# Start-up, v loads and low parts moved in a one-core attention and MLP kernel

## The chip, the cores and the metric

The kernel runs on one core of one Trainium2 chip. The metric is the device time of one execution in microseconds (us): the median over several runs. The engines of the core run side by side, each through its own queue in order: TensorE (PE, with its weight loads as PEld), VectorE (DVE), ScalarE (ACT), GpSimd (POOL) and SyncE (SP, which here only issues transfers, DMAs). They wait for one another by semaphores.

## What is computed

64 heads (8 batches of 8) of causal attention with a decay, of 576 positions and 64 dimensions each, then an MLP with a squared ReLU over the 4608 rows that result.

```python
scores = scale * np.matmul(q, k.transpose(0, 1, 3, 2))
log_f = np.log(np.clip(f, 0.0001, 1.0))
cum = np.cumsum(log_f, axis=-1)
decay = cum[:, :, :, None] - cum[:, :, None, :]
scores = np.where(causal, -1000000000.0, scores + decay)
scores = scores - np.max(scores, axis=-1, keepdims=True)
attn = np.exp(scores)
attn = attn / (np.sum(attn, axis=-1, keepdims=True) + 1e-09)
attn_out = np.matmul(attn, v)
x = attn_out.transpose(0, 2, 1, 3).reshape(B * S, H * D)
h = np.maximum(x @ w_in, 0.0)
out = h * h @ w_out                    # w_in 512 x 2048, w_out 2048 x 512
```

All of it is wanted in float32. The query's own sum `cum[q]` cancels in the softmax, so only the key's sum is carried, as extra rows of the operand k.

## The kernel before

**Heads and slots.** Each head is cut in six units (`UNITS`), a block of up to 128 keys by a stretch of queries. A slot is one unit of one head, and the main loop (`for n in range(-2 * NU, last_slot + 1)`) writes a slot at a time: the unit's scores, the product with v of the unit two slots back (`av_part`), then what the tables `events` and `fins` hold for this slot and its two halves, and between them a share of the MLP (`fill`) and of the weights' conversion (`cv`). `in_order` then binds PE, ACT, DVE and POOL to the order in which the instructions were written; SP's transfers after the start-up follow it too, each behind those before it.

**Row maxima.** Softmax needs each query's maximum before its scores are raised. Six maximum units per head (`max_units`) run one head ahead of the scores: a matmul over q and k rounded to float32r (`r2`, `kl0`, 66 rows: 64 dimensions and the high and low half of the sums), then a reduction on DVE out of the same PSUM bank (L384). `MAXIMA` gives their slots. For heads 0 to 9 (`NWHOLE`) the maxima are turned by TensorE and copied as a row of the whole float32 operand `whole` (tile `rl`) by ACT (`turn_maxima`, L411); the scores of these heads are plain float32 matmuls (L423). From head 10 on the scores are two float32r matmuls (L425, L428) of a rounded part (tile `rk`) and a low part (tile `rl`), made by `prep` in four parts. In heads 10 to 19 DVE subtracts the low parts (L329 for k, L333 for q), from head 20 on POOL does.

**The banks.** Maximum units and scores share PSUM banks. While the MLP's first chunks run, the maxima have no banks of their own and take turns with the scores, for a time on two banks; a second maximum unit then cannot start before DVE has read the first.

**Sums.** `decay` clips f, takes Ln on ACT, sums along each of 64 rows by one DVE scan (L167), rounds the sums to `ch` (L170) and subtracts for `cl` (L171). Head 0's two rows go from there into its two operands by transfers (L284); all 64 heads' rows go to DRAM (`cum_dr`, L176), and every later head loads its two rows from there (L286).

**Start-up.** PE runs 36 matmuls on a constant (`spin`, L768) until there is work; their result is not used. SP loads f, head 0's q and k (`rl`), a first weight tile. POOL's queue loads q and k of heads 0 and 1 a second time as float32r (`rk`, L292, which rounds them), and fills constant rows.

**Loads.** v of head h is loaded one head ahead (slot 2 of head h-1) into one of three buffers, and is first used in slot 2 of head h (L487). Weights come in 32 tiles of 512 KB, DEPTH 4 ahead of their conversion, which ACT and DVE share (L206, L211 on ACT; L230, L235, L238, L242, L217 on DVE). `RATES` says how many conversion steps a slot gets: 0.67 in the first slots before head 0, none in the last six of them, 0.93 and then 1.8 once heads run.

Of the kernel before, what the change touches and what calls it, by code (L numbers as in the profile page):

```python
# [9 lines left out]
F32 = mybir.dt.float32  # L10
# [4 lines left out]
ALU = mybir.AluOpType  # L15
# [19 lines left out]
def decay_attention_relu2_kernel(  # L35
# [77 lines left out]
    nc.vector.memset(turn[:, P:P + 2 * CW].bitcast(F32), 0.0)  # L113
    nc.vector.tensor_copy(out=eye_r, in_=eye)

# [37 lines left out]
    cum, cums = [], []  # L153

    def load_f():
        nc.sync.dma_start(out=fr[:NH, 0, :], in_=f)

    def decay():
        ft, zt, ct = (fr[:NH, i, :] for i in range(3))
        nc.vector.memset(zt, 0.0)  # L160
        constant_rows(nc.vector, rounded[0])
        nc.vector.tensor_scalar(ft, ft, 1e-4, 1.0, ALU.max, ALU.min)
        nc.scalar.activation(out=ft, in_=ft, func=AF.Ln)
        warm_exp = wk.tile([P, 8], F32, name="tcol")
        nc.vector.memset(warm_exp[:, :1], 0.0)
        nc.scalar.activation(out=warm_exp[:, :1], in_=warm_exp[:, :1], func=AF.Exp)
        nc.vector.tensor_tensor_scan(ct, zt, ft, 0.0, ALU.add, ALU.add)  # L167
        chl = wk.tile([P, 2, S], F32R, name="qkraw", bufs=1)
        ch, cl = chl[:, 0, :], chl[:, 1, :]
        nc.vector.tensor_copy(out=ch[:NH], in_=ct)  # L170
        nc.vector.tensor_tensor(out=cl[:NH], in0=ct, in1=ch[:NH].bitcast(F32), op=ALU.subtract)  # L171
        cum.extend(x.bitcast(F32) for x in (ch, cl))
        cums.append(chl[:NH].bitcast(F32))
# [105 lines left out]

    def load_cum(h, k, r=D):  # L280

        if h == 0:
            for i, c in enumerate(cum):
                nc.sync.dma_start(out=f32(k[r + i:r + i + 1, :S]), in_=c[h:h + 1])  # L284
        else:
            nc.sync.dma_start(out=f32(k[r:r + 2, :S]), in_=cum_dr[h])  # L286

# [7 lines left out]

    def load_whole(h):

        x = state[h]["whole"] = whole[h % 2]
        nc.sync.dma_start(out=x.raw[:D], in_=qk[h])
        if cum:  # L300
            load_cum(h, x.k, D + 1)
# [368 lines left out]

    RATES = (0.67, 0, 0.93, 1.8)
    LAG = 2
# [72 lines left out]
    for h in range(NH):  # L745
        split = h >= NWHOLE
        if split:
            at((h - 2) * NU + LOAD, 0, load, h)
            for part in range(4):
                at((h - 1) * NU + SPLIT[part], 1, prep, h, part)  # L750
        else:
            if h > 1:
                at((h - 3) * NU + 3, 0, load_rounded, h)
                at((h - 2) * NU + 5, 1, load_whole, h)
        at((h - 1) * NU + VLOAD, 1, load_v, h)
        at((h - 1) * NU + VSPLIT, 1, split_v, h)
        for i, x in enumerate(MAXIMA[split]):
            at((h - 1) * NU + int(x), int(2 * x) % 2, max_unit, h, i)
        if not split:
            at((h - 1) * NU + (4 if h else 3), 0, turn_maxima, h)  # L760
# [9 lines left out]
    for i in range(12):  # L770
        at(i // 2 - NU, i % 2, spin, 1)
    spin(36)
    load_f()
    load_rounded(0)
    load_whole(0)
    constants()
    convert(1)
    decay()
    load_cum(0, rounded[0].k)
    load_cum(0, whole[0].k, D + 1)  # L780
    store_cum()
    convert(1)
    load_rounded(1, False)
    load_whole(1)
    load_cum(1, rounded[1].k)
    start = {i.name for i in tc.nc.cur_bb.bb.instructions}
    for n in range(-2 * NU, last_slot + 1):
# [15 lines left out]
        for do in events.get((n, 0), ()):  # L803
            do()
        wr = RATES[0] * (n < -NU) if n < -NU // 2 else RATES[1 if n < 0 else 2 if n < ready[0] else 3]
        cv(wr / 2)
# [50 lines left out]
```

## Time and profile before

| what | us |
|---|---|
| runs of the kernel | 1206.62, 1206.76, 1213.95 |
| median | 1206.76 |
| the profiled execution's own time | 1208.21 |
| its span, first to last instruction | 1206.5 |

The profile's page gives the busy time of each engine and its share of the span. The view of the waits has one row per pair of a waiting line and the one that released it: us in total, times, longest. The timeline has a row per instruction or run of like instructions: start, duration, engine, line, operation, out<-in, count, and in brackets the idle time before it with what ended it. A view of windows gives, for each stretch of the span, its length, each engine's busy time and count, then PEclk (the granted TensorE clock as a share of full speed), the busy share of the transfer engines, and GB/s. "L376" is a line of the kernel before; a step whose line moves keeps its name in words.

### The profile page before, as it was taken

Reading aid. Unit: us, or ns where it says so; the run is one execution under the profiler, and the core shown is the slowest. Engines: PE = TensorE matmul, PEld = TensorE weight load, DVE = VectorE, ACT = ScalarE, POOL = GpSimd, SP = SyncE. Lnnn points to the kernel's source line nnn. Section 1 sums busy time; section 2 is a strip of 40 time slices with the busy share of each in tenths; the row PEclk is TensorE's granted clock in tenths of the full one; section 3 lists DMA queues with packets and bytes.
Section 4 is the critical chain, followed back from the end, with each engine's and each line's share of the span. In section 5 each row is a group of like instructions: output and inputs, shape, how many; then the busy total and the mean of one; then the engine's idle time right before and its main releaser. Section 6 shows DMA issues by size and latency. Waiting matters only on the chain. (4 is left out here: it accounts for less than half of the span.)

```text
span 1206.5 us, 23195 instructions
## 1 busy us (share of the span) xinstructions
PE 1178.1 (98%) x7786; PEld 1040.9 (86%) x7786; DVE 784.9 (65%) x2096; ACT 684.6 (57%) x1716; POOL 316.9 (26%) x511
## 2 busy tenths in 40 slices
PE   8999999999999999999999999999999999999998
PEld 4667877789998989899999899988999899999997
DVE  5889987766766676666656667666666766543332
ACT  3765555546666566656565566666566666533232
POOL 2110000213434343422222343334333434200000
PEclk9999999999999999999999999999999999999999
DMA  7785722221212121111110212112121112000000
GB/s 204 194 209 165 196 54 46 74 67 35 51 42 60 42 55 43 50 42 35 36 50 17 59 38 54 38 43 59 42 54 36 47 42 59 12 28 18 1 19 18
DMA packets 109798, 73.33 MB, mean 61 GB/s; under 512 B 90720, under 2 KB 90720, under 8 KB 109680
## 3 DMA queue, kind: packets, MB, share of 16 engines
q1 hardware_dynamic: 108880, 68.90, 22.4%
q0 software_dynamic: 800, 2.95, 1.1%
q8 instruction: 62, 1.02, 0.4%
q14 instruction: 56, 0.46, 0.1%
HBM read 58.71 MB, written 9.87 MB: 57 GB/s over the span
## 5 line engine op out<-in xcount | busy, mean ns | idle before, releaser
L621 PE MATMUL bank<-w,gh 128*128 128x512 f32 x1152 | 413.5, 399 | 0.0
L591 PE MATMUL bank<-xh,w 128*128 128x256 f32 x2304 | 331.6, 286 | 5.3 <-ACT r L606 5.1
L591 PEld LDWEIGHTS bank<-xh,w 128*128 128x128 f32 x2304 | 300.1, 189 | 16.8 <-ACT r L606 9.3
L456 DVE TENSOR_TENSOR pl<-p,ph 128x320 fp32r<-128x320 f32 (+4 forms) x288 | 175.4, 610 | 200.6 <-ACT ph L455 195.1
L621 PEld LDWEIGHTS bank<-w,gh 128*128 128x128 f32 x1152 | 217.5, 189 | 37.9
L621 PE MATMUL bank<-w,gl 128*128 128x512 f32 x576 | 227.1, 394 | 0.2 <-DVE gl L609 0.2
L455 ACT CAST ph<-p 128x320 fp32r<-128x320 f32 (+4 forms) x288 | 119.4, 415 | 162.0 <-POOL p L442 119.2
L607 DVE TENSOR_TENSOR g<-r 128x256 f32<-128x256 f32 x288 | 124.3, 432 | 102.0 <-ACT r L606 101.7
L442 POOL TENSOR_SCALAR_AFFINE_SELECT p<-p 128x128 f32<-128x128 f32 (+1 forms) x240 | 85.9, 358 | 396.1 <-ACT p L440 328.2
L606 ACT ACTIVATE r<-bank 128x256 f32<-128x256 f32 x288 | 109.7, 381 | 137.1 <-PE bank L591 124.5
L591 PE MATMUL bank<-xl,w 128*128 128x256 f32 x1152 | 184.8, 283 | 0.0
L440 ACT ACTIVATE p<-bank 128x320 f32<-128x320 f32 (+4 forms) x288 | 111.2, 386 | 117.9 <-PE bank L428 105.9
L384 DVE CUSTOM_DVE_ANT_0 bank<-bank,mz 128x256 f32<-128x256 f32 (+4 forms) x320 | 133.6, 431 | 50.6 <-PE bank L376 50.2
L609 DVE TENSOR_TENSOR gl<-g,gh 128x256 fp32r<-128x256 f32 x288 | 139.1, 483 | 34.4 <-PE bank L621 1.0
L591 PEld LDWEIGHTS bank<-xl,w 128*128 128x128 f32 x1152 | 158.5, 191 | 0.2 <-DVE xl L577 0.2
L608 ACT ACTIVATE gh<-r 128x256 fp32r<-128x256 f32 x288 | 120.4, 418 | 9.2
L376 PE MATMUL bank<-rk 66*128 66x320 f32 (+4 forms) x384 | 109.1, 314 | 13.4 <-DVE tcol L384 8.4
L621 PEld LDWEIGHTS bank<-w,gl 128*128 128x128 f32 x576 | 109.2, 190 | 15.0 <-DVE gl L609 1.7
L428 PE MATMUL bank<-rl 128*128 128x320 f32 x324 | 95.1, 294 | 0.0
L425 PE MATMUL bank<-rk 67*128 67x320 f32 x324 | 93.4, 288 | 0.0
L376 PEld LDWEIGHTS bank<-rk 66*128 66x128 f32 (+1 forms) x384 | 67.1, 181 | 30.4 <-DVE tcol L384 12.8
L466 PE MATMUL bank<-pl,vh 128*65 128x320 f32 (+4 forms) x336 | 91.3, 272 | 0.0
(97 smaller groups left out, 1478.8 us busy)
## 6 DMA issues: line engine op xcount, KB each, us to landing
qkraw<-in_qk SPq DMA_DIRECT2D x54, 288.0 KB
v<-in_v SPq DMA_DIRECT2D x64, 160.0 KB
out<-osb SPq DMA_DIRECT2D x36, 256.0 KB
den<-rdr SPq DMA_DIRECT2D x62, 144.0 KB
w<-in_w_in SPq DMA_DIRECT2D x16, 512.0 KB
w<-in_w_out SPq DMA_DIRECT2D x16, 512.0 KB
rk<-tcol SPq DMA_DIRECT2D x216, 0.5 KB
rl<-in_qk SPq DMA_DIRECT2D x10, 288.0 KB
```

Of the source, the lines that this page charges most:

```text
L376: nc.tensor.matmul(ps[:m, :n], st["r2"][:D + 2, q0:q0 + m], st["kl0"][:D + 2, k0:k0 + n], start=True, stop=True,)
L384: nc.vector.tensor_tensor_reduce(out=ps[:m, :n], in0=ps[:m, :n], in1=mz[:m, mo:mo + n], op0=ALU.add, op1=ALU.min, scale=-1.0, scalar=init, ...
L428: nc.tensor.matmul(ps[:kn, :n], st["l2"][:, k0:k0 + kn], st["r1"][:, q0:q1], start=False, stop=not added,)
L440: nc.scalar.activation(out=p[:kn, :n], in_=ps[:kn, :n], func=AF.Exp, scale=SCALE)
L455: nc.scalar.copy(out=ph[:kn, :n], in_=p[:kn, :n])
L456: nc.vector.tensor_tensor(out=pl[:kn, :n], in0=p[:kn, :n], in1=ph[:kn, :n].bitcast(F32), op=ALU.subtract,)
L591: nc.tensor.matmul(ph[:, :T], w[:, s, cc], x[:, cc, :], start=(cc == 0 and k == 0), stop=(cc == NCC - 1 and k == 2),)
L606: nc.scalar.activation(out=r, in_=ph[:, :T], func=AF.Relu)
L607: nc.vector.tensor_tensor(out=g, in0=r, in1=r, op=ALU.mult)
L608: nc.scalar.activation(out=gh, in_=r, func=AF.Square)
L609: nc.vector.tensor_tensor(out=gl, in0=g, in1=gh.bitcast(F32), op=ALU.subtract)
L621: nc.tensor.matmul(po, g[:, ts], w[:, s], start=(fc == 0 and k == 0), stop=(fc == NF - 1 and k == 2),)
```

## The change

Five things are changed.

1. *Head 0's start.* q and k of head 0 are no longer loaded twice; ACT rounds them out of the float32 tile (two copies of 64 rows). f is loaded on 66 partitions: ACT's queue brings head 0's row twice more, onto partitions 64 and 65. The clip, Ln, scan and rounding run on 66 partitions, and one DVE operation on the last two writes head 0's two sum rows in place: `ch * sign + sum`, with sign 0 on partition 64 (the sum, rounded on writing) and -1 on 65 (its low half).
2. *Head 1's sums* and head 0's float32 rows come from chip by transfers, not through DRAM.
3. *Fewer spins*: 20 for 36. The rounding of the unit matrix `eye_r` stands behind the clip. Conversion steps that stood before head 0's maxima stand behind them (RATES 0 until three slots before head 0, then 1.0).
4. *v sooner*: heads 2 to 9 load v two heads ahead in place of one.
5. *Maxima ahead of low parts*: for heads from 10 on, where a maximum unit and a part of `prep` fall in the same half slot, the maximum unit is now written first.

```diff
-    nc.vector.tensor_copy(out=eye_r, in_=eye)
...
+    NR = NH + 2
+    signs = wk.tile([P, 8], F32, name="tcol")[:, :1]
...
         nc.sync.dma_start(out=fr[:NH, 0, :], in_=f)
+        nc.scalar.dma_start(out=fr[NH:NR, 0, :], in_=f[0:1].broadcast_to([2, S]))
 
     def decay():
-        ft, zt, ct = (fr[:NH, i, :] for i in range(3))
+        ft, zt, ct = (fr[:NR, i, :] for i in range(3))
+        x = rounded[0]
...
+        nc.vector.memset(signs[NH:NR], -1.0)
+        nc.vector.memset(signs[NH:NH + 1], 0.0)
         nc.vector.tensor_scalar(ft, ft, 1e-4, 1.0, ALU.max, ALU.min)
         nc.scalar.activation(out=ft, in_=ft, func=AF.Ln)
+        nc.vector.tensor_copy(out=eye_r, in_=eye)
+        nc.scalar.copy(out=x.k[:D, :S], in_=whole[0].k[:D, :S])
+        nc.scalar.copy(out=x.q[:D], in_=whole[0].q[:D])
...
-        nc.vector.tensor_copy(out=ch[:NH], in_=ct)
-        nc.vector.tensor_tensor(out=cl[:NH], in0=ct, in1=ch[:NH].bitcast(F32), op=ALU.subtract)
+        nc.vector.tensor_copy(out=ch[:NR], in_=ct)
+        nc.vector.scalar_tensor_tensor(
+            x.k[NH:NR, :S], ch[NH:NR].bitcast(F32), signs[NH:NR], ct[NH:NR], ALU.mult, ALU.add,
+        )
+        nc.vector.tensor_tensor(
+            out=cl[:NH], in0=ct[:NH], in1=ch[:NH].bitcast(F32), op=ALU.subtract,
+        )
...
-    RATES = (0.67, 0, 0.93, 1.8)
+    RATES = (1.0, 0.93, 1.8)
...
-            for part in range(4):
-                at((h - 1) * NU + SPLIT[part], 1, prep, h, part)
...
-        at((h - 1) * NU + VLOAD, 1, load_v, h)
+        if h:
+            at((h - (2 if 1 < h < NWHOLE else 1)) * NU + VLOAD, 1, load_v, h)
         at((h - 1) * NU + VSPLIT, 1, split_v, h)
         for i, x in enumerate(MAXIMA[split]):
             at((h - 1) * NU + int(x), int(2 * x) % 2, max_unit, h, i)
+        if split:
+            for part in range(4):
+                at((h - 1) * NU + SPLIT[part], 1, prep, h, part)
...
-    spin(36)
+    spin(20)
     load_f()
-    load_rounded(0)
-    load_whole(0)
+    state[0] = dict(r2=rounded[0].q, kl0=rounded[0].k, p={})
+    load_rounded(1, False)
+    load_whole(0, False)
+    convert(1)
     constants()
+    decay()
+    for i, c in enumerate(cum):
+        for x, r in (whole[0], D + 1), (rounded[1], D):
+            h = 0 if x is whole[0] else 1
+            nc.sync.dma_start(out=f32(x.k[r + i:r + i + 1, :S]), in_=c[h:h + 1])
     convert(1)
-    decay()
-    load_cum(0, rounded[0].k)
-    load_cum(0, whole[0].k, D + 1)
+    load_v(0)
+    load_whole(1, False)
+    load_cum(1, whole[1].k, D + 1, False)
     store_cum()
     convert(1)
-    load_rounded(1, False)
-    load_whole(1)
-    load_cum(1, rounded[1].k)
...
-        wr = RATES[0] * (n < -NU) if n < -NU // 2 else RATES[1 if n < 0 else 2 if n < ready[0] else 3]
+        wr = 0 if n < -NU // 2 else RATES[0 if n < 0 else 1 if n < ready[0] else 2]
```

PE's own order is the same in both kernels but for the 16 spins. On the others it moves. DVE at the start, before (`p` is the tile of the unit matrix, `xt` holds f and its sums, `rk` the rounded operand, `qkraw` the two halves of the sums):

```order
L114 CAST p<-p 128x128
L160 MEMSET xt_86 64x576
L141 MEMSET rk_79 32x576
L142 MEMSET rk_79 32x578
L143 MEMSET rk_79 64x2
L148 MEMSET rk_79 2x2
L162 TENSOR_SCALAR xt_86<-xt_86 64x576
L165 MEMSET tcol 128x1
L167 SCALAR_TENSOR_TENSOR xt_86<-xt_86 64x576
L170 CAST qkraw<-xt_86 64x576
L171 TENSOR_TENSOR qkraw<-xt_86,qkraw 64x576
L230 TENSOR_SCALAR wmag<-wmag 128x512
```

and DVE at the start now:

```order
L142 MEMSET rk_78 64x2
L147 MEMSET rk_78 2x2
L166 MEMSET tcol 2x1
L167 MEMSET tcol 1x1
L168 TENSOR_SCALAR xt_85<-xt_85 66x576
L170 CAST p<-p 128x128
L174 MEMSET tcol 128x1
L176 SCALAR_TENSOR_TENSOR xt_85<-xt_85 66x576
L179 CAST qkraw<-xt_85 66x576
L180 SCALAR_TENSOR_TENSOR rk_78<-qkraw,tcol,xt_85 2x576
L183 TENSOR_TENSOR qkraw<-xt_85,qkraw 64x576
L398 ISA bank_166,tcol<-bank_166,mz 128x256
```

The unit matrix went from the head of the queue to behind the clip, the two-row operation (L180) is new, and the weight's steps (L230 before) left the place between the sums and the first maximum (L398 is the reduction, L384 before). SP's queue at the start, before:

```order
L284 DMA rk_79<-qkraw 1x16x36 x2
L284 DMA rl<-qkraw 1x16x36 x2
L176 DMA cum_dr<-qkraw 64x1152
L195 DMA w_164<-in_w_out 128x1024
L299 DMA rl<-in_qk 64x1152
L286 DMA rl<-cum_dr 2x576
L286 DMA rk_80<-cum_dr 2x576
L306 DMA v<-in_v 128x5x64
L286 DMA rk_79<-cum_dr 2x576
```

and SP's queue at the start now:

```order
L799 DMA rl<-qkraw 1x16x36
L799 DMA rk_79<-qkraw 1x16x36
L799 DMA rl<-qkraw 1x16x36
L799 DMA rk_79<-qkraw 1x16x36
L209 DMA w_154<-in_w_out 128x1024
L320 DMA v<-in_v 128x5x64
L313 DMA rl<-in_qk 64x1152
L300 DMA rl<-qkraw 1x16x36 x2
L190 DMA cum_dr<-qkraw 64x1152
L209 DMA w_233<-in_w_in 128x1024
L209 DMA w_235<-in_w_out 128x1024
L297 DMA rk_78<-cum_dr 2x576
```

Head 1's rounded operand (`rk`) now gets its sums in the first four transfers rather than from DRAM behind a weight tile and q and k; the store to DRAM has gone back behind v, and the first load from it (L297) is head 2's. DVE in one of the heads 10 to 19, before:

```order
L607 TENSOR_TENSOR g<-r 128x256
L609 TENSOR_TENSOR gl<-g,gh 128x256
L329 TENSOR_TENSOR rl<-qkraw,rk_80 64x576
L384 ISA bank_2776,tcol<-bank_2776,mz 128x256
L384 ISA tcol 128x1
L384 ISA bank_2789,tcol<-bank_2789,mz,tcol 128x320
```

and the same place now:

```order
L621 TENSOR_TENSOR g<-r 128x256
L623 TENSOR_TENSOR gl<-g,gh 128x256
L398 ISA bank_2764,tcol<-bank_2764,mz 128x256
L398 ISA tcol 128x1
L343 TENSOR_TENSOR rl<-qkraw,rk_79 64x576
L398 ISA bank_2779,tcol<-bank_2779,mz,tcol 128x320
```

The low part of k (L329, now L343) stands between the first and the second maximum unit, where it stood ahead of both.

More of the change, by code (lines that the diff above doesn't have):

```diff
@@ L153, in decay_attention_relu2_kernel @@
     cum, cums = [], []
+    NR = NH + 2
+    signs = wk.tile([P, 8], F32, name="tcol")[:, :1]
     def load_f():
         nc.sync.dma_start(out=fr[:NH, 0, :], in_=f)
+        nc.scalar.dma_start(out=fr[NH:NR, 0, :], in_=f[0:1].broadcast_to([2, S]))
     def decay():
-        ft, zt, ct = (fr[:NH, i, :] for i in range(3))
+        ft, zt, ct = (fr[:NR, i, :] for i in range(3))
+        x = rounded[0]
         nc.vector.memset(zt, 0.0)
-        constant_rows(nc.vector, rounded[0])
+        constant_rows(nc.vector, x)
+        nc.vector.memset(signs[NH:NR], -1.0)
+        nc.vector.memset(signs[NH:NH + 1], 0.0)
         nc.vector.tensor_scalar(ft, ft, 1e-4, 1.0, ALU.max, ALU.min)
         nc.scalar.activation(out=ft, in_=ft, func=AF.Ln)
+        nc.vector.tensor_copy(out=eye_r, in_=eye)
+        nc.scalar.copy(out=x.k[:D, :S], in_=whole[0].k[:D, :S])
+        nc.scalar.copy(out=x.q[:D], in_=whole[0].q[:D])
         warm_exp = wk.tile([P, 8], F32, name="tcol")
@@ L278, in load, with load_cum @@
         raws[h] = raw
-    def load_cum(h, k, r=D):
-        if h == 0:
+    def load_cum(h, k, r=D, stored=True):
+        if stored:
+            nc.sync.dma_start(out=f32(k[r:r + 2, :S]), in_=cum_dr[h])
+        else:
             for i, c in enumerate(cum):
                 nc.sync.dma_start(out=f32(k[r + i:r + i + 1, :S]), in_=c[h:h + 1])
-        else:
-            nc.sync.dma_start(out=f32(k[r:r + 2, :S]), in_=cum_dr[h])
     def load_rounded(h, rows=True):
@@ L294, in load_rounded, with load_whole @@
             load_cum(h, x.k)
-    def load_whole(h):
+    def load_whole(h, rows=True):
         x = state[h]["whole"] = whole[h % 2]
         nc.sync.dma_start(out=x.raw[:D], in_=qk[h])
-        if cum:
+        if cum and rows:
             load_cum(h, x.k, D + 1)
```

## The prediction

> **What bounds the kernel now.** I read the page first, then the waits of TensorE, the windows by stage, the timeline of the start, and last the timeline around each wait.
>
> ```profile
> span 1206.5 us, 23195 instructions
> PE 1178.1 (98%) x7786; PEld 1040.9 (86%) x7786; DVE 784.9 (65%) x2096; ACT 684.6 (57%) x1716; POOL 316.9 (26%) x511
> PE bank L376 <- DVE tcol L384: 8.4, 8, 1.7
> PE bank L591 <- ACT r L606: 5.1, 8, 0.8
> PE bank L376 <- DMA rk<-cum_dr: 2.6, 1, 2.6
> PE bank L487 <- DMA v<-in_v: 2.0, 1, 2.0
> PE bank L487 <- ACT w L211: 1.2, 1, 1.2
> 27.00:77.00 50.00, 45.91 (x266) 31.22 (x265) 39.84 (x123) 39.15 (x95) 6.58 (x14) 1.00 0.79 191
> 97.00:262.00 165.00, 154.77 (x974) 129.71 (x973) 135.25 (x344) 90.44 (x219) 14.92 (x33) 0.99 0.38 103
> 262.00:1035.00 773.00, 767.53 (x5241) 701.22 (x5240) 519.32 (x1408) 475.12 (x1210) 280.55 (x423) 1.00 0.19 45
> ```
>
> TensorE is busy 1178.1 of 1206.5 us; its order stays as it is but for 16 spins, so the change can win only its idle 28.4 us, clock, and the time before its first useful matmul. From 262 us on it idles 5.5 us in 773, and nothing there is touched on its path. What can move lies in three places: the start, the early heads (4.1 us idle in 27 to 77), and heads 10 to 19 (10.2 us idle in 97 to 262, 8.4 of them maxima waiting for DVE).
>
> **The start.**
>
> ```profile
> 0.81 1.28 ACT L163 ACT_TABLE_LOAD   x1 [0.81 <-PEq L847]
> 1.70 9.89 PE L768 MATMUL bank<-mz 128*128 128x448 bf16 x36 [1.70 <-POOL mz L95]
> 2.47 0.54 DVE L160 MEMSET xt<- 64x576 f32 x1
> 4.58 0.63 DVE L162 TENSOR_SCALAR xt<-xt 64x576 f32<-64x576 f32 x1
> 5.24 0.68 ACT L163 ACTIVATE xt<-xt 64x576 f32<-64x576 f32 x1 [3.15 <-DVE tcol L165]
> 5.96 1.35 DVE L167 TENSOR_TENSOR_SCAN xt<-xt 64x576 f32<-64x576 f32 x1 [0.74 <-ACT xt L163]
> 7.34 0.47 DVE L170 CAST qkraw<-xt 64x576 fp32r<-64x576 f32 x1
> 7.62 3.52 PEld L768 LDWEIGHTS <-mz 128*128 128x128 bf16 x19 [0.22 <-issue]
> 7.84 1.31 SPq L284 DMA_DIRECT2D rk<-qkraw  x2
> 7.84 0.75 DVE L171 TENSOR_TENSOR qkraw<-xt,qkraw 64x576 fp32r<-64x576 f32 x1
> 8.04 0.68 ACT L206 ACTIVATE wmag<-w 128x512 f32<-128x512 f32 x1 [0.60 <-DMA w<-in_w_in]
> 11.74 0.35 PE L376 MATMUL bank<-rk 66*128 66x256 f32 x1 [0.15 <-DMA rk<-qkraw]
> 14.57 0.23 SPq L286 DMA_DIRECT2D rk<-cum_dr  x1
> 16.44 0.70 PE L423 MATMUL bank<-rl 67*128 67x320 f32 x2
> 19.73 0.50 PE L376 MATMUL bank<-rk 66*128 66x256 f32 x2 [2.59 <-DMA rk<-cum_dr]
> 27.73 0.67 PE L376 MATMUL bank<-rk 66*128 66x256 f32 x2
> 34.85 0.67 PE L376 MATMUL bank<-rk 66*128 66x256 f32 x2
> 2.00:3.00 1.00, 1.00 (x4) 0.46 (x3) 0.75 (x2) 0.09 (x1) 0.95 (x3) 1.00 0.91 198
> 7.00:8.00 1.00, 1.00 (x5) 0.39 (x4) 0.93 (x3) 0.43 (x2) 0.78 (x7) 1.00 0.12 14
> ```
>
> The first maximum starts at 11.74, when head 0's sum rows land, 3.1 us after the second of two transfers was issued (its half of 1.31 us begins when L171 ends, 8.59). Now DVE writes these rows. When, is a chain. VectorE no longer waits for the unit matrix first, so its four fills, begun at 2.47 before, begin at about 1.1; from there to the clip it took 4.58 - 2.47 = 2.1, and two tiny fills more make it free at about 3.5. f must have landed: its 147 KB lead the queue, at 198 GB/s from 2.0 they are through by 2.75, and w's transfer, whose bytes end by about 7.1 (the share falls to 0.12), lands at 8.04, 0.9 later. So f lands at about 3.65, and before 4.58 in any case. The extra row pair on ScalarE's queue is tiny and lands with it. A wait is added here: ScalarE now waits for f ahead of Ln's table load, which ran at 0.81 for nothing before. So 3.65, table 1.28, Ln 0.68, scan 1.35, rounding 0.47, the two-row operation, with gaps of 0.03: 7.54 before that operation. No row shows it; by length it lies between L170 (0.47) and L171 (0.75), both 576 long; I take 0.75 as it has two tensor operands like L171: 8.3. Two rows for 64 save nothing, since I take time by length. With f at 4.55 it is 9.2.
>
> ScalarE's two roundings of q and k have Ln's form, 0.68 each: from 5.65 to 7.0, if head 0's float32 q and k are in. They stand behind f in the queue (442 KB, 5 us); shared evenly with w they land with it, 8.0, and the roundings end at 9.4. Exp's table and the weight's first step follow on ScalarE, which is next needed 3.8 us after the first maximum.
>
> The spins: 19 weight loads in 3.52 is 0.19 each, so 16 fewer end 3.0 earlier, at 8.6. That is later than 8.3, so the first maximum starts at 8.6 to 8.75 and gains **3.0**; bounds 2.3 (9.4) and 3.1. The unit matrix (DVE's wait for Ln covers it) and the three conversion steps behind head 0's maxima (they run while TensorE turns the maxima and scores, 16.44 to 19.73 before) cost nothing; without that cover they would delay head 1's first reduction by up to 1.5. One reload of 295 KB on POOL's queue is gone.
>
> Then 4.7 us of maxima, as 11.74 to 16.44: first score at 13.45. Its float32 rows and head 1's come by four transfers issued from 7.5 to 10.7; at 3.1 each the last lands by 13.1. Head 1's maxima, which waited 2.59 for a row from DRAM, follow the score at 14.1 without a wait: **2.6**; bounds 1.5 and 2.6.
>
> SP has the store and the read from DRAM further back, so head 2 pays instead: its row is issued once w, v, q and k, two sums and the store are through, about 17.7 by the issue times and some 250 GB/s. A row like it took 5.1 (issued 14.57, used 19.73): 21 to 22.8, when head 2's maxima want it at 14.1 + 7.1 = 21.2 (a head takes 34.85 - 27.73 = 7.1). I charge **0.7**; bounds 0 and 1.6. Head 1's v, three weight tiles behind, lands just about when wanted, and is in this charge.
>
> **The clock.**
>
> ```profile
> 21.50:24.50 3.00, 3.00 (x12) 2.00 (x11) 2.89 (x12) 1.41 (x4) 0.91 (x2) 0.50 0.62 204
> 243.50:246.50 3.00, 3.00 (x14) 2.76 (x13) 1.08 (x6) 0.80 (x2) 0.00 (x0) 0.50 0.03 0
> ```
>
> For some 3.4 us each TensorE has half its clock, the only two such stretches. Each follows a wait, of 2.59 us (ended 19.73) and of 1.62 (below). Head 1 took 27.73 - 19.73 = 8.0 against 7.1, so the first costs 0.9; the second lies in a stretch without idle and costs up to 1.7. If the waits cause them, both go: I take **0.9** and **1.0** (it may come back at another wait); bounds 0 and 2.6. The Trainium skill, "TensorE: Matmul & The Clock Gate", Part 1, "What's actually happening", has the clock halved only after an idle window of about 3.4 us. By that rule neither wait was enough and the drops need not go; the sum would be less by these 1.9. The trace shows drops after shorter waits, but also the 2.0 us wait for v without one.
>
> **v sooner.**
>
> ```profile
> 45.91 0.72 PE L487 MATMUL bank<-ph,v 128*65 128x320 f32 x2 [1.18 <-ACT w L211]
> 62.84 0.59 SPq L306 DMA_DIRECT2D v<-in_v  x1
> 70.50 0.72 PE L487 MATMUL bank<-ph,v 128*65 128x320 f32 x2 [2.01 <-DMA v<-in_v]
> ```
>
> Both are the first use of a head's v. v took 7.7 us from 62.84. The first is put down to ScalarE, whose p it needs was done sooner; I read it as v too. A head more (7.1 us) covers both: 3.2. The buffer it takes was last read one slot before, so SP waits little, but sum rows, weights and q, k queue behind it. They stay in the same order, a head's work apart. Transfers are 79% busy in this stage and get 3 us less for it, so q and k may be the next to be late. I take **2.9**; bounds 1 and 3.2.
>
> **Maxima ahead of low parts.**
>
> ```profile
> 157.12 0.75 DVE L333 TENSOR_TENSOR rl<-qkraw,rk 64x576 fp32r<-64x576 f32 x1
> 158.31 0.24 PE L376 MATMUL bank<-rk 66*64 66x64 f32 x1 [0.97 <-DVE tcol L384]
> 190.84 0.41 PE L376 MATMUL bank<-rk 66*128 66x320 f32 x1 [0.68 <-DVE tcol L384]
> 222.21 0.84 DVE L329 TENSOR_TENSOR rl<-qkraw,rk 64x576 fp32r<-64x576 f32 x1
> 223.50 0.42 PE L376 MATMUL bank<-rk 66*128 66x320 f32 x1 [1.75 <-DVE tcol L384]
> 242.65 0.42 PE L376 MATMUL bank<-rk 66*128 66x320 f32 x1 [1.62 <-DVE tcol L384]
> ```
>
> At 223.50 TensorE waited 1.75 for a bank; the reduction that frees it stood behind the low part of k, 0.84. Now it comes first, and the wait is shorter by that. At 158.31 it is the same with q's low part. At 190.84 no low part stood ahead, so that 0.68 stays. Seven of the eight waits are of the first kinds; one is 0.2: 6 x 0.75 + 0.2 = 4.7. The low part is needed in the next head's first slot, two and more slots off, so its delay is free; it now delays the second reduction, which a third unit may wait for. I take **4.2**; bounds 1.5 and 4.7. From head 20 on low parts run on POOL and ScalarE, and no such waits are left to win.
>
> **The sum.** 3.0 + 2.6 - 0.7 + 0.9 + 2.9 + 4.2 + 1.0 = 13.9. The profiled execution took 1208.21, 1.7 more than its span, and would take 1194.3; the median of the runs, 1206.76, lies 1.45 below it, so I forecast 1192.9.
>
> **Rivals.**
> - The start gives little: f or q and k land late, the table load behind f counts in full, and head 2's row costs 1.6. Then the start gives 2.3 + 1.5 - 1.6 = 2.2 in place of 4.9 and its clock drop moves along (0.9): 1196.5. For it: four steps rest on landing times that no row shows. Against: the spins leave 0.3 us of room.
> - The low part only moves the wait on to the third unit: 1.5 for 4.2, and the clock at 243 stays: 1196.6. For it: DVE is busy 82% there (135.25 of 165). Against: after the second unit TensorE has MLP work to do.
> - The clock's halving does not hang on the waits: both drops stay, 1192.9 + 0.9 + 1.0 = 1194.8. For it: the 2.0 us wait at 70.50 has no drop behind it. Against: nowhere else is there one. The Trainium skill's rule above, "TensorE: Matmul & The Clock Gate", would have it so.
> - Slower than before: in heads 2 to 9 transfers become the bound, as v comes ahead of rows and q, k. It decides once each of the eight heads loses more than 13.9 / 8 = 1.75 us; at 3.5 each it gives 1206.8 + 14 = 1221. Against: 0.79 of 50 us is 39.5 us of transfers under 45.9 of matmuls.
>
> **How the numbers follow.** My case 0.46, the start 0.20, the low part 0.17, the clock 0.14, slower 0.03. A measurement of this kernel can tell about 1%, 12 us, from no change: faster is below 1194.7. My case runs from 1190.5 (4.7, 3.2, no charge, 1.7 for the second drop) to 1195.5, nine tenths of it below; the clock's case lies on the line, a half; of the other two, a quarter, where v and the rest give their upper ends. That is 0.41 + 0.07 + 0.09: faster 0.57, within 1% 0.40, slower 0.03. The range takes in the first two rivals with 3 us for their spread, and 1 us below my case for waits on ScalarE (L591, 5.1 us) that may shrink too: 1189.5 to 1199.5.
>
> **What would show it.** Right: the first maximum near 8.7 on a spin's end, the first score near 13.4, no wait for head 1's row, clock 1.00 from 21 to 25, no wait at a head's first product with v up to 77 us, waits of L376's line for DVE down from 8.4 to about 4. Wrong: TensorE idle after the last spin, a wait for a DRAM row near 21, waits for q and k between 27 and 77, or a half clock at another place.

## The result, and the profile after

The change took 1202.74 us (median of 11 runs, 1198.96 to 1206.03) beside 1208.14 us for the kernel before (11 runs, 1206.10 to 1218.05): a ratio of 0.9942, 95% interval 0.9922 to 0.9961. Run again on another chip (e13 below) it was 0.9952 (0.9931 to 0.9973). It is faster by 5.2 to 5.4 us in the medians, and by 0.5 to 0.6% (6 to 7 us) in the ratios, which compare means. Both intervals lie below 1, so about half of the 12 us that I called the limit could be told. The time is 9.8 us above the 1192.9 that was forecast.

A correction to the text ahead of the prediction: SP's transfers after the start-up are bound only to stand behind the start-up's last one; the scheduler sets their order among themselves.

The profiled execution of the change took 1206.03 us, the longest of its eleven, so its trace overstates the losses. The page's span and busy times, and the waits of TensorE (waiting line, releaser: us in total, times, longest):

```profile
span 1204.3 us, 23168 instructions
PE 1177.4 (98%) x7770; PEld 1041.7 (87%) x7770; DVE 783.2 (65%) x2099; ACT 686.0 (57%) x1718; POOL 318.5 (26%) x510
PE bank L605 <- ACT r L620: 5.4, 8, 0.8
PE bank L390 <- DVE tcol L398: 4.3, 7, 1.0
PE bank L390 <- DMA rk<-cum_dr: 3.0, 1, 3.0
PE bank L390 <- DVE rk L358: 2.9, 4, 1.0
PE bank L437 <- DMA rl<-cum_dr: 1.8, 1, 1.8
PE bank L390 <- ACT tcol L175: 1.6, 1, 1.6
PE bank L501 <- DMA v<-in_v: 0.7, 1, 0.7
```

L390 is the line of the maxima (L376 before), L437 the whole scores (L423), L501 the products with v (L487). The two waits for v (2.0, and the 1.2 put down to ScalarE) are gone, and those for DVE's reductions shrank as meant, from 8.4 to 4.3. The 0.7 for v is new: it is head 0's v, for which the kernel before did not wait. Two rows from DRAM are waited for, 3.0 at head 2 (2.6 at head 1 before) and 1.8 at head 7. The timeline shows where the start's gain went:

```profile
1.70 5.22 PE L784 MATMUL bank<-mz 128*128 128x448 bf16 x20 [1.70 <-POOL mz L95]
3.67 0.58 DVE L168 TENSOR_SCALAR xt<-xt 66x576 f32<-66x576 f32 x1 [0.34 <-DMA xt<-in_f]
7.56 0.81 DVE L180 SCALAR_TENSOR_TENSOR rk<-qkraw,tcol,xt 2x576 fp32r<-2x576 f32 x1
8.52 0.35 PE L390 MATMUL bank<-rk 66*128 66x256 f32 x1 [1.60 <-ACT tcol L175]
13.62 0.59 SPq L190 DMA_DIRECT2D cum_dr<-qkraw  x1
13.66 0.67 PE L390 MATMUL bank<-rk 66*128 66x256 f32 x2
16.44 0.72 PE L501 MATMUL bank<-ph,v 128*65 128x320 f32 x2 [0.72 <-DMA v<-in_v]
19.06 0.30 SPq L297 DMA_DIRECT2D rk<-cum_dr  x1
24.51 0.57 PE L390 MATMUL bank<-rk 66*128 66x256 f32 x2 [3.04 <-DMA rk<-cum_dr]
34.75 0.67 PE L390 MATMUL bank<-rk 66*128 66x256 f32 x2
```

The row at 8.52 names an activation on ScalarE (L175, ended 8.48). VectorE's two-row operation had ended just before, at 8.37, and it is the one waited for: in e13 the first maximum began at 8.40, 0.15 after that operation and before L175 ended (8.51).

The first maxima of heads 0 to 3 start at 8.52, 13.66, 24.51 and 34.75; before it was 11.74, 19.73, 27.73 and 34.85. The change is 6.07 us ahead at head 1 and 0.10 ahead at head 3. Between them 0.72 went to head 0's v, 3.04 to head 2's row, and 3.1 to the clock: heads 2 to 3 took 10.24 us where a head takes 7.1, 0.9 of it balanced by the clock drop that the kernel before had there. 6.07 - 0.72 - 3.04 - 3.1 + 0.9 = 0.1.

The windows of the change (length, busy time and count of PE, PEld, DVE, ACT and POOL, PEclk, share of the transfer engines, GB/s) show an idle window at full clock, and behind it three windows of half clock. Their edges are those of a grid that is explained with e13 to e15:

```profile
21.33:24.74 3.41, 0.37 (x3) 0.26 (x3) 0.00 (x0) 1.23 (x4) 0.00 (x0) 1.00 1.03 239
24.74:28.15 3.41, 3.41 (x12) 2.39 (x12) 1.51 (x6) 1.01 (x3) 0.11 (x1) 0.51 1.08 250
72.53:75.94 3.41, 3.41 (x10) 2.05 (x9) 2.36 (x8) 1.71 (x4) 0.00 (x0) 0.51 0.40 100
82.77:86.18 3.41, 3.41 (x11) 2.12 (x10) 2.20 (x7) 2.44 (x6) 0.00 (x0) 0.51 0.87 245
```

With the second window of the first stretch (28.15 to 31.57) and one more at 239.8, the change's profile has 17 us of half clock, and that of the kernel before has 6.8.

From head 3 to head 12 the change falls back from 0.10 us ahead to 0.82 behind: both waits for v (3.2 us) are gone, but a wait of 1.80 for a row has come, and two windows of half clock cost 1.7 each. Together these would lose 2.0 us where 0.9 were lost; the difference is not traced. Heads 12 to 19, where the low parts moved, came out as forecast. The first maximum of heads 12 and 19, in the change:

```profile
134.62 0.28 PE L390 MATMUL bank<-rk 66*128 66x256 f32 x1
257.12 0.28 PE L390 MATMUL bank<-rk 66*128 66x256 f32 x1
```

and before:

```profile
133.80 0.28 PE L376 MATMUL bank<-rk 66*128 66x256 f32 x1
260.50 0.28 PE L376 MATMUL bank<-rk 66*128 66x256 f32 x1
```

126.70 us became 122.50: 4.2 us. Of the 3.38 us that the change is ahead at head 19, 1.8 are lost again by head 34, most of it where TensorE waits for a rounding on DVE (L358: 2.9 us, 1.3 before). This wait varies without the change too: the kernel before with unused matmuls in its start (e12) waited 2.5 us for the same line, the change with such matmuls (e14) 1.5.

### The profile page after: what moved, and what is told of

It is laid out like the page before. It is cut to its first block, busy times and chain, and to the rows that moved or that the text cites. A ratio compares the mean times of both kernels' runs of the same rounds, so it can differ in the third digit from the quotient of the medians.

```text
span 1204.3 us, 23168 instructions
## 1 busy us (share of the span) xinstructions
PE 1177.4 (98%) x7770; PEld 1041.7 (87%) x7770; DVE 783.2 (65%) x2099; ACT 686.0 (57%) x1718; POOL 318.5 (26%) x510
## 5 line engine op out<-in xcount | busy, mean ns | idle before, releaser
L470 DVE TENSOR_TENSOR pl<-p,ph 128x320 fp32r<-128x320 f32 (+4 forms) x288 | 172.3, 599 | 200.7 <-ACT ph L469 197.1
L621 DVE TENSOR_TENSOR g<-r 128x256 f32<-128x256 f32 x288 | 128.7, 447 | 101.5 <-ACT r L620 101.5
L398 DVE CUSTOM_DVE_ANT_0 bank<-bank,mz 128x256 f32<-128x256 f32 (+4 forms) x320 | 133.6, 432 | 51.4 <-PE bank L390 50.2
L623 DVE TENSOR_TENSOR gl<-g,gh 128x256 fp32r<-128x256 f32 x288 | 130.2, 452 | 33.3
L390 PE MATMUL bank<-rk 66*128 66x320 f32 (+4 forms) x384 | 110.7, 319 | 12.7 <-DVE tcol L398 4.3
L390 PEld LDWEIGHTS bank<-rk 66*128 66x128 f32 (+1 forms) x384 | 67.9, 184 | 29.5 <-DVE tcol L398 8.1
```

What stands on the lines that cost most here:

```text
L390: nc.tensor.matmul(ps[:m, :n], st["r2"][:D + 2, q0:q0 + m], st["kl0"][:D + 2, k0:k0 + n], start=True, stop=True,)
L398: nc.vector.tensor_tensor_reduce(out=ps[:m, :n], in0=ps[:m, :n], in1=mz[:m, mo:mo + n], op0=ALU.add, op1=ALU.min, scale=-1.0, scalar=init, ...
L470: nc.vector.tensor_tensor(out=pl[:kn, :n], in0=p[:kn, :n], in1=ph[:kn, :n].bitcast(F32), op=ALU.subtract,)
L621: nc.vector.tensor_tensor(out=g, in0=r, in1=r, op=ALU.mult)
L623: nc.vector.tensor_tensor(out=gl, in0=g, in1=gh.bitcast(F32), op=ALU.subtract)
```

## The experiments

Of each kernel the granted clock is known for every execution, so each has two figures: the median, and the time at full clock. The latter comes from a least-squares fit of time on lost clock (one less the mean granted clock), with one slope for all kernels and one constant for each, over 280 executions of 17 kernels and repeats: 1.17 us per 0.001, differences good to 0.8 to 1.1 us (95%) if the one slope holds for all. Fitted alone, e5 has a slope of 1.01 and e6 of 0.87; with their high lost clock their figures are the least sure. Two of e1's executions, of 2278.83 us and of a recorded clock of 0.943 at 1202.39 us, are left out of it. Ratios are to the kernel before on the same chip.

| run | median us | ratio, 95% interval | mean lost clock | at full clock, to before |
|---|---|---|---|---|
| before (118 executions) | 1208.5 | | 0.0050 | 1203.3 |
| the change | 1202.74 | 0.9942 (0.9922 to 0.9961) | 0.0045 | -6.1 |
| e5 start alone | 1207.85 | 0.9988 (0.9971 to 1.0006) | 0.0073 | -4.5 |
| e3 v alone | 1209.17 | 0.9996 (0.9972 to 1.0020) | 0.0058 | -0.7 |
| e4 maxima first alone | 1205.23 | 0.9954 (0.9925 to 0.9983) | 0.0043 | -3.5 |
| e8 without v sooner | 1201.57 | 0.9943 (0.9922 to 0.9963) | 0.0040 | -5.6 |
| e1 head 2's sums from chip | 1202.17 | 0.9941 (0.9914 to 0.9967) | 0.0066 | -8.4 |
| e7 two weight tiles later | 1202.73 | 0.9950 (0.9928 to 0.9972) | 0.0043 | -6.0 |
| e6 e1 and head 0's v sooner | 1205.34 | 0.9971 (0.9958 to 0.9985) | 0.0079 | -7.7 |
| e10 e1, e6 and e7 together | 1202.34 | 0.9927 (0.9898 to 0.9956) | 0.0049 | -7.4 |
| e2 row's wait filled | 1201.23 | 0.9924 (0.9896 to 0.9952) | 0.0033 | -6.1 |
| e9 both waits filled | 1196.69 | 0.9906 (0.9872 to 0.9940) | 0.0018 | -7.7 |
| e11 e1, v's wait filled | 1201.76 | 0.9942 (0.9921 to 0.9963) | 0.0043 | -6.3 |
| e12 before, its wait filled | 1207.20 | 0.9982 (0.9964 to 1.0001) | 0.0038 | 0.0 |
| e13 the change again | 1202.28 | 0.9952 (0.9931 to 0.9973) | 0.0054 | -6.6 |
| e14 e9 again, beside e13 | 1198.67 | 0.9924 (0.9901 to 0.9948) | 0.0022 | -6.3 |
| e15 same products elsewhere | 1205.62 | 0.9980 (0.9956 to 1.0004) | 0.0053 | -4.2 |

### The parts alone

**e5: the start alone.** The change with parts 4 and 5 undone.

```diff
-            at((h - (2 if 1 < h < NWHOLE else 1)) * NU + VLOAD, 1, load_v, h)
+            at((h - 1) * NU + VLOAD, 1, load_v, h)
...
         if split:
             at((h - 2) * NU + LOAD, 0, load, h)
+            for part in range(4):
+                at((h - 1) * NU + SPLIT[part], 1, prep, h, part)
...
-        if split:
-            for part in range(4):
-                at((h - 1) * NU + SPLIT[part], 1, prep, h, part)
```

> The changed kernel's start-up alone: v one head ahead and the low parts ahead of the maxima, as before. The runs so far, brought to full clock (1.25 us for each 0.001 of lost clock), put the change at 6.0 us, maxima first alone at 3.4 and v alone at 0.6. Theory (the parts add up, and the start's 6 us up to head 1 are halved again by the wait for head 2's row): 2.0 us less than before at full clock, about 1200.8, and the wait for head 2's row of 2.5 to 3.5 us is there again. Rival (the start keeps what it wins and the other parts lose it): 5 to 6 us less, about 1197.

A timeline row of e5 shows the same wait for head 2's row as in the change:

```profile
24.26 0.82 PE L390 MATMUL bank<-rk 66*128 66x256 f32 x2 [3.20 <-DMA rk<-cum_dr]
```

At full clock it is 4.5 us faster, between the 2.0 of the theory and the 5 to 6 of the rival (3.3 with its own slope). Its lost clock rose from 0.0050 to 0.0073, which is 2.7 us, so the ratio is only 0.12% below 1, and its interval reaches beyond.

**e3: v alone**, in the kernel before.

```diff
-        at((h - 1) * NU + VLOAD, 1, load_v, h)
+        at((h - (2 if 1 < h < NWHOLE else 1)) * NU + VLOAD, 1, load_v, h)
```

> The kernel before with v two heads ahead for heads 2 to 9 and nothing else. Theory of the prediction: both waits for v (1.18 and 2.01 us) go and nothing is late next, heads 2 to 9 shorten by 2.9 us, ratio 0.9976. Rival (as the changed kernel's trace shows, head 7's float32 sum row is the next to be late): a wait of 1 to 2 us for the row of the whole operand near 72 us, so a gain of 1 to 1.5 us.

No wait for v is left, but two others have come, at the first score of a head:

```profile
62.60 0.78 PE L423 MATMUL bank<-rl 67*128 67x320 f32 x2 [0.89 <-ACT pl L440]
78.00 0.78 PE L423 MATMUL bank<-rl 67*128 67x320 f32 x2 [0.83 <-ACT pl L440]
```

The view puts them down to ScalarE, but the operation that it names had ended 0.4 us before, at 62.18 in the first case. What TensorE waited for is q and k of that head, issued seven us before:

```profile
55.52 0.48 SPq L299 DMA_DIRECT2D rl<-in_qk  x1
61.80 0.38 ACT L440 ACTIVATE pl<-bank 128x256 f32<-128x256 f32 x1
```

By the trace's semaphore records this transfer landed at 62.51, and the one issued at 69.97 at 77.91, each 0.06 us ahead of TensorE's first weight load. So another transfer became late, as the rival said, but q and k and not the row. 0.7 us is left of 3.2 us of waits, within the uncertainty of nothing.

**e8: the change without part 4**, that is with the first line of e5's edit alone.

> The changed kernel with v one head ahead for all heads, as before. Theory (sooner v wins what the waits for v cost, less the wait for the sum row that came in its place): waits for v come back in heads 3 to 7, 1 to 3 us in total, and the time at full clock is 0.6 to 1.5 us above the changed kernel's 1196.9. Rival (sooner v does nothing or harms): 1196.9 or less.

Its profile waits three times for v, 4.9 us in all. One is head 0's, of 2.49; the other two are those of the kernel before, now as long as this:

```profile
48.64 0.72 PE L501 MATMUL bank<-ph,v 128*65 128x320 f32 x2 [1.04 <-DMA v<-in_v]
71.95 0.72 PE L501 MATMUL bank<-ph,v 128*65 128x320 f32 x2 [1.39 <-DMA v<-in_v]
```

Undoing v sooner costs 0.5 us at full clock, with an uncertainty of 1.3, and nothing in the median. In the change the place of 71.95 is taken by a wait of 1.80 us at 71.91 for the next thing in the queue, head 7's rows (the L437 row above). With e3's q and k that makes v the first of several transfers that came late together, not the bound.

**e4: maxima first alone**, part 5 in the kernel before (the diff of the change has it).

> The kernel before with the maximum units written ahead of the low parts and nothing else. Theory: waits of the maxima for DVE fall from 8.4 to 4.2 us, and head 20 starts 4.2 us earlier against head 10 than before, ratio 0.996 to 0.9965. Rival (the wait only moves to the third unit): 1.5 us.

3.5 us at full clock, near the theory's 4.2 and well above the rival's 1.5. The waits of L376 for DVE fell from 8.4 to this, less far than the 4.2 that was expected:

```profile
PE bank L376 <- DVE tcol L384: 6.0, 7, 1.3
```

Two of the seven were longer than in the change, 1.15 for 0.18 and 1.27 for 0.63.

### What is late next in the start

**e1: head 2's sums from chip too**, so that no row of the start goes through DRAM.

```diff
-            load_cum(h, x.k)
+            load_cum(h, x.k, stored=h > 2)
```

> The changed kernel, but head 2's two rounded sum rows are sent from chip right behind the store, instead of being read back from DRAM once the store has landed. Theory (the row is late because of the store's round trip): the wait of 3.04 us before head 2's first maximum falls below 0.5 us, head 2 starts at 21 to 22 us instead of 24.5, and if the halved clock behind it is a consequence of the wait, head 3 starts at 28.5 to 29.5 instead of 34.75; time 3 to 6 us less than the changed kernel's 1202.7, so 1197 to 1200. Rival (the start is bound by the amount of bytes, whatever row comes from where): another load is late by about as much, head 3 starts at 33 or later and the time stays within 1 us of 1202.7.

The wait for the row is gone, and head 0's v, 0.72 late in the change's profile, is now this late:

```profile
18.15 0.93 PE L501 MATMUL bank<-ph,v 128*65 128x320 f32 x2 [2.42 <-DMA v<-in_v]
```

That isn't e1's making alone: in e13, the change itself, v was 2.18 late. At full clock e1 is 2.3 us faster than the change (uncertain by 1.1). It loses more clock (0.0066), and the medians are the same, as the rival said.

**e7: two weight tiles later.** The staging of weights runs 2 tiles ahead in place of 4 for the first three, to leave the queue to v and the rows.

```diff
-            while len(staged) < min(i + 1 + DEPTH, NW):
+            while len(staged) < min(i + 1 + (DEPTH if i > 2 else 2), NW):
```

> The changed kernel with weight tiles 2 ahead instead of 4 until four are converted, so that two tiles (1 MB) leave the first 25 us; head 2's row still comes through DRAM. Theory (the round trip, not the bytes): the store still lands at 18 to 19 us, the row is issued at about 19 and lands in 3 to 5 us, so the wait at head 2 is 1.5 to 3 us. Rival (bytes: the row waits behind 1 MB of weights): the row lands in under 2.5 us and the wait is below 1 us; time at full clock about 1194.5.

No difference in time, and neither text had the wait: v's was 2.37 at 18.21 in its profile, and none for the row stood behind it. SP again waited 3.0 us for the store to land before it issued the row, at 19.60.

**e6: e1 with v of head 0 ahead of the second weight tile.**

```diff
-    convert(1)
     load_v(0)
+    convert(1)
```

> The changed kernel with head 2's rows from chip, and head 0's v issued ahead of the second weight tile instead of behind it. Theory (each of the start's waits is one transfer's place in SP's queue): the wait for v at 15.7 us (0.7 to 2.4 in the runs so far) falls below 0.3, no wait of over 1 us stands before 40 us, and at full clock the time is 1193.5, 0.9 less than with the rows alone (1194.4). Rival (the bytes of the first 20 us bound it): another load is late by the same amount and the time stays at 1194.4 or above.

Head 0's v is in time. Head 1's v is next, and later than either, so the rival came; at full clock the time is 1195.7:

```profile
26.34 1.30 PE L501 MATMUL bank<-ph,v 128*65 128x320 f32 x2 [3.47 <-DMA v<-in_v]
```

**e10: e1, e6 and e7 together.**

> Head 2's rows from chip, head 0's v ahead of the second weight tile, and two weight tiles (1 MB) out of the first 25 us, all three in the changed kernel. With the first two alone head 1's v was the next to be late, by 3.5 us. Theory (what the start wins is bounded by the bytes that it wants: each wait removed makes the next transfer late until bytes are taken out): now no wait of over 1 us for a transfer before 40 us, and at full clock 1192 to 1194, against 1197.3 for the changed kernel and 1195.8 without the tiles. Rival (some fixed delay, not bytes): another wait of 2 to 3.5 us before 30 us, and 1195 or above at full clock.

Now no wait of over 1 us for a transfer is left before 40 us (0.62 for sum rows at 21.77), then 1.76 at 59.14 for q and k. But TensorE waits 1.69 at 19.53 and 0.77 at 26.66 for exponentials on ScalarE, which stood behind the conversion of the weight tiles that now come late:

```profile
18.60 0.66 ACT L220 ACTIVATE wmag<-w 128x512 f32<-128x512 f32 x1 [3.29 <-DMA w<-in_w_out]
25.54 0.66 ACT L220 ACTIVATE wmag<-w 128x512 f32<-128x512 f32 x1 [4.30 <-DMA w<-in_w_in]
```

It is no faster than the change in the median, and 1195.9 at full clock, where the theory had 1192 to 1194. In e6 and e10 transfers brought forward left another late, and TensorE waited 3.5 and 1.7 us for it or for what it held up. The transfer engines are full in this stretch (a share of 1.03 and 1.08 in the windows above). That the amount of bytes is the bound fits this, but isn't shown: e7 took 1 MB out and won nothing.

### The clock

**e2: the wait for head 2's row filled** with 16 products on zeros, whose bank nothing reads.

```diff
+    def fill_wait():
+        ps = bank("m")
+        for _ in range(16):
+            nc.tensor.matmul(ps[:, :MW], mz[:, :P], mz, start=True, stop=True)
+
+    at(NU, 0, fill_wait)
```

> The changed kernel with 16 unused matmuls (3.0 us) put into TensorE's order ahead of head 2's first maximum, so that TensorE works through the wait for the row. Theory (the clock is halved because TensorE sat idle): the row still lands at about 24.5, but the half clock from 25 to 31.7 is gone, and head 3 starts near 31.7 instead of 34.75; time about 3 us less, 1199.7. Rival (the clock's halving does not hang on that wait): half clock in the same place, head 3 at 34.7, time within 1 us of 1202.7.

The half clock still came, at 16.7 us in its profile: in that execution v was 1.90 us late at 17.57, ahead of the filled place. So it decides nothing between the two texts. Two of its eight executions ran at full clock, 1195.76 and 1199.27 us.

**e9: both waits filled**, with 10 products ahead of the first product with v and 8 ahead of head 2's first maximum (`fill_wait` now takes a number).

```diff
+    at(1, 1, fill_wait, 10)
+    at(NU, 0, fill_wait, 8)
```

> The changed kernel with unused matmuls ahead of both waits of the start: 10 (1.9 us) before the first product with v, 8 (1.5 us) before head 2's first maximum. In all ten profiled executions so far the first stretch of half clock began during the first wait of 1.6 us or more for a transfer, or up to 2 us behind it; the run that filled only head 2's wait still had 1.9 us idle for v. Theory (idle time at the start takes the clock away): no wait of over 1 us before 30 us, no half clock before 40 us in the profile, lost clock 0.0015 on average instead of 0.0045 over the runs, median 1198.5 to 1200. Rival (the half clock comes whatever TensorE does): half clock of 3.4 to 17 us before 40 us as in the others, lost clock 0.004 or more, median 1202 to 1203.

The theory came: 1196.69 us, the fastest of all kernels here, at a lost clock of 0.0018, and in the profile no half clock before 81.9 us.

**e11: e1 with 12 such products** ahead of the first product with v.

> The change, with head 2's two-row operands too from the chip, and with 12 useless products on zeros (nothing reads their bank) set on TensorE ahead of the first product with v, where the run without them waited 2.42 us. Theory that TensorE's idle waits take the clock: no wait over 1.6 us is left up to that product, so the first half-clock stretch does not come before 40 us unless head 1's half of v is late (3.47 us late where v came one half sooner); lost clock 0.002, time 1196 to 1197.5 us. Theory that the stretch comes whatever TensorE waits for: lost clock stays 0.004 to 0.007, 1200 to 1203 us.

The time and the lost clock (0.0043) are the rival's. Its mechanism isn't shown: up to 33 us there was no half clock, and it then followed two waits within 5 us, for head 1's v, which the theory had excepted, and for head 2's q and k:

```profile
26.58 0.72 PE L501 MATMUL bank<-ph,v 128*65 128x320 f32 x2 [1.44 <-DMA v<-in_v]
31.59 0.78 PE L437 MATMUL bank<-rl 67*128 67x320 f32 x2 [1.33 <-DMA rl<-in_qk]
```

**e12: the kernel before with 14 products** in its wait for head 1's row, `at(0, 0, fill_wait, 14)`.

> The kernel before, with 14 useless products on zeros (nothing reads their bank) set on TensorE ahead of head 1's first maximum, where it waits 2.62 us for that head's row. Theory that the idle wait takes the clock: the half-clock stretch at 21 to 25 us is gone, lost clock falls from 0.005 to 0.002 and the time from 1208.6 to 1204.5 to 1206 us. Theory that the clock's loss hangs on other things: lost clock stays near 0.005, and the time within 1 us of the kernel before.

The drop at 21 us is gone (a window of the profile, 20.14 to 23.56, at clock 1.00), and the lost clock fell less than expected, to 0.0038. The time is 1207.20, between what the two theories said, its interval just reaching 1. The wait's own 2.6 us were not won, as the products filled it.

**e13, e14, e15: the change, e9 again, and e9's 18 products where nothing waits**, on one chip. e15 sets them behind head 2's first maxima:

```diff
-    at(1, 1, fill_wait, 10)
-    at(NU, 0, fill_wait, 8)
+    at(NU + 3, 0, fill_wait, 10)
+    at(NU + 4, 0, fill_wait, 8)
```

> The change itself, beside the two runs that follow it on one chip. Both theories: 1201 to 1204 us, mean lost clock 0.004 to 0.005, waits of about 3.0 us at head 2's row in the profile.

> The change with 10 useless products ahead of the first product with v and 8 ahead of head 2's first maximum, once more, on the same chip as the change. Theory that TensorE's idle waits in the start take the clock: lost clock 0.002 to 0.003, 4 to 6 us faster than the change on this chip. Theory that the earlier 1196.7 us was that chip's or that hour's clock: lost clock like the change's, and at most 2 us faster (the wait for the row shortened).

> The change with the same 18 useless products set three and four slots later, behind head 2's first maxima, where TensorE waits for nothing; both start waits stay. Theory that idle waits take the clock: lost clock like the change's (0.004 to 0.005), and the products' own 18 x 0.19 = 3.4 us on top where they hide under no later wait: 1203 to 1207 us. Theory that more products on TensorE early on keep the clock up wherever they stand: lost clock 0.002 to 0.003, and about 1200 us.

e14 took 3.6 us less than e13 (95% interval of the means 1.1 to 6.1), a little under what was expected. At full clock the two are alike (1197.0 and 1196.8), so the gain is all clock: 0.0054 to 0.0022, a difference of 0.0032 (0.0012 to 0.0052). e15 lost as much clock as e13, and its products cost it 2.4 us at full clock. So it is not products as such that keep the clock up, but products where TensorE waited.

The trace shows why some waits cost clock and others don't. The windows of e13 around its wait for v (2.18 us, ended 17.78; against what was expected, the row of head 2 was not waited for):

```profile
13.72:17.13 3.41, 1.88 (x11) 1.26 (x9) 2.71 (x9) 1.65 (x4) 0.00 (x0) 1.00 1.09 235
17.13:20.54 3.41, 2.76 (x9) 1.80 (x10) 1.23 (x7) 0.73 (x2) 0.51 (x1) 0.50 0.90 354
```

of e14 at the same place:

```profile
12.59:16.00 3.41, 3.41 (x19) 2.11 (x17) 2.32 (x8) 1.83 (x5) 0.00 (x0) 1.00 1.06 269
16.00:19.41 3.41, 3.41 (x21) 2.23 (x19) 2.27 (x10) 1.06 (x3) 0.52 (x1) 1.00 1.01 350
```

and of e15:

```profile
14.88:18.29 3.41, 1.34 (x8) 0.86 (x8) 2.14 (x7) 1.21 (x3) 0.00 (x0) 1.00 1.07 249
18.29:21.71 3.42, 3.42 (x13) 1.82 (x12) 3.08 (x9) 0.83 (x3) 0.51 (x1) 0.52 1.05 336
```

The clock changes only at steps of 3.413 us. Their phase is seen in the first microseconds, when the spins' weight loads turn from one in 0.37 us to one in 0.19; in the change that was here:

```profile
4.26 2.21 PEld L784 LDWEIGHTS <-mz 128*128 128x128 bf16 x12 [0.22 <-issue]
```

It was at 7.62 in the profile before, 6.89 in e13, 5.76 in e14. Counted from that moment, every one of the 34 drops up to 290 us in the 17 profiles begins a whole number of steps later, to within a tenth of a step: the change's at 6.02, 20.02, 23.02 and 69.02 steps, before's at 4.00 and 69.01.

So I cut all 17 profiles into such windows up to 290 us and took the share in which TensorE was not busy. Of the windows that ran at full clock with half or more idle, 15 of 15 were followed by half clock; with 0.3 to 0.5 idle, 12 of 34; with less, 7 of 1264. Those seven all end at 80 to 84 us and hold the ten products of L555, which move a single element each, 1.27 us in all, and so count as busy here with little work in them. That is a pointer and no proof: every profile has two such batches, and most have no drop behind them. The windows also answer what was open in the prediction, the wait of 2.01 us for v at 70.50 that had no drop behind it. First its window in the kernel before, then the one ahead of that kernel's first drop:

```profile
69.06:72.47 3.41, 1.97 (x11) 1.32 (x12) 1.99 (x10) 1.31 (x4) 0.69 (x2) 1.00 0.94 170
17.86:21.27 3.41, 1.54 (x9) 1.30 (x10) 0.97 (x5) 0.40 (x2) 0.00 (x0) 1.00 1.08 351
```

1.97 of 3.41 busy (0.42 idle) kept the clock, as 22 of the 34 windows with 0.3 to 0.5 idle did; 1.54 (0.55 idle), in the window that ended behind the wait for head 1's row, lost it. Since the phase differs from run to run, a wait of about 2 us loses the clock in some executions and not in others.

## Why the prediction was wrong

The forecast was 13.9 us of gain on 1206.76, the median of three runs. Over 118 executions the kernel before has a median of 1208.5, so 1.8 us of any forecast against that figure were the sample's. The gain came out at 5.4 in the medians and 6.1 to 6.6 at full clock, where the terms without the clock had been 12.0. The rows marked "in the trace" are read from the two profiles.

| term | forecast | measured |
|---|---|---|
| first maximum earlier | 3.0 | 3.2 (11.74 to 8.52) |
| head 1's row without DRAM | 2.6 | 2.9 (6.07 at head 1, less 3.2) |
| head 2's row, with head 1's v in its charge | -0.7 | -3.0 in the trace, no wait for head 1's v |
| head 0's v | no term | -0.7 in the trace |
| first clock drop gone | 0.9 | -2.2 in the trace (0.9 - 3.1) |
| v sooner | 2.9 | 0.5 to 0.7 at full clock (e8, e3) |
| maxima first | 4.2 | 4.2 in the trace, 3.5 alone (e4) |
| second clock drop gone | 1.0 | 0: it is there at 239.8, and in e13 and e15 |

- **The first maximum and head 1: right**, and the chain was right step by step: f at 3.67 (forecast 3.65), the two-row operation at 7.56 in 0.81 (7.54, 0.75). ScalarE's roundings of q and k ended at 6.97, well before the 9.4 that I had. The spins' end, which I took for the limit at 8.6, came at 6.92; VectorE's operation set the start.
- **"I charge 0.7; bounds 0 and 1.6": the step that failed first.** The time at which the row was wanted was right, 24.51 - 3.04 = 21.5 against 21.2. The issue was 1.4 us later than the 17.7 I worked out, and the row took 5.45 to its use, a little over the 5.1 of the row I had. So it came at 24.51, beyond the 21 to 22.8 whose middle I charged. The issue was late because of the store ahead of it. From 15.92 SP waited for it to land:

```profile
SPq L297 <- DMA cum_dr<-qkraw: 3.1, 1, 3.1
```

  From its issue at 13.62 the store took 5.4 us; in the kernel before it took 3.4 (10.86 to 14.21), and SP waited 1.2 for it. More than the size, the charge was wrong in kind. It held head 2's row and head 1's v, and head 0's v had no term at all, though the change left it 4.7 us from its issue (10.98) to its use (wanted at 15.72) where the kernel before had 6.8 (14.84 to 21.61). It was late by 0.72 in the change's profile and by 1.9 to 2.5 in those of e2, e7, e8, e13 and e15. So the start has a queue of transfers with little slack, not one late row. The rival "the start gives little" put the start's terms at 2.2, and the trace has 3.2 + 2.9 - 3.0 - 0.7 = 2.4; but that is in part luck, as it had f or q and k late and neither was. e5 at full clock, 4.5, would speak for the forecast's 4.9 instead. That is the least sure of the figures, and in the median on its chip e5 is 0.6 us ahead.
- **The clock: right that waits cost it, wrong that the waits would go.** I took both drops as gone because their two waits were mended, and put no drop behind the wait that I charged myself. The second drop stayed although its wait shrank from 1.62 to 0.95: with 0.48 for a rounding beside it, its window was still 0.42 idle. At full clock the change wins 6.1; its lost clock, 0.0045 and 0.0054 in its two series, is that of the kernel before, 0.0050, so the 1.9 us of these two terms came out as nothing. The rival that the halving doesn't hang on waits is refuted by e14 and e15.
- **"A head more covers both: 3.2 ... I take 2.9": mis-sized about fourfold**, and below my own lower bound of 1, though that lies within the uncertainty. I had named the reason: transfers were 79% busy there and "q and k may be the next to be late". They were in e3, 0.89 and 0.83 us; in the change it was a row, 1.80. I took only 0.3 off for it.
- **Maxima first: right**, and the rival that the low part only moves the wait on fell: 4.2 against 1.5.

The parts alone sum to 8.7 us at full clock (4.5, 0.7, 3.5) where the whole wins 6.1 to 6.6. The difference of 2.4 is uncertain by 1.5, so part of it can be noise; what the rest is stays open.

## What to carry to other kernels

- Where several transfers share a saturated stretch, mending the wait that shows wins only the distance to the next transfer, here 0.5 us out of 3 for v, and at the start 2.3 of the 6.1 that the change was ahead at head 1. Forecast the landing of the whole queue, and charge the next one as soon as it has less slack than what is being won.
- A wait of TensorE costs twice where it fills half of a clock window: its own time, and 1.7 us for each window of half clock behind it. If the wait can't be removed, useless products in it keep the clock; with 18 of them the change became 1196.7 and 1198.7 us, ratio 0.9906 (0.9872 to 0.9940) and 0.9924 (0.9901 to 0.9948), better than both kernels.
- Before the sizes of small parts are compared, put the time against the granted clock of each execution: the spread of some 15 us within one kernel is mostly that (1.3 us about the fitted line).

## What the runs showed of the hardware that was not expected

- The grid of 3.413 us and the limit near half a window, above. The Trainium skill, "TensorE: Matmul & The Clock Gate", Part 1, "What's actually happening", states a free-running window of 3413 ns, and the traces agree in all 34 drops. It also has the clock fall after an idle window of about 3.4 us; here windows with 0.31 to 0.55 idle were enough, so by the measurement no whole window has to be idle. That rule, as I read it in the prediction, would have kept the clock at full in e13, where a wait of 2.18 us took it.
- The half clock lasted 1 to 5 windows (3.4 us in the kernel before, 17.1 in e13), with TensorE busy throughout the later ones. What ends it is open.
- The same 20 spins at the start took 5.22 us in the change's profile, 6.49 in e13's and 5.97 in e14's, as the fast phase began at 4.26, 6.89 and 5.76. So the first maximum's room was 1.60 us in one execution and 0.2 in another.
- With one order of transfers, different transfers came late in different executions: v by 0.72 and the row by 3.04 in one profile of the change, v by 2.18 and the row not at all in the other.
